# Moving the operands of the matmuls to other SBUF addresses modulo 256 bytes

## The chip, the cores and the metric

The kernel runs on one core of one Trainium2 chip. The metric is device time in microseconds (us) from one launch, lower is better. Three runs of the kernel before gave 332.88, 333.24 and 334.3 us, median 333.24. The profile shows one further execution, which took 333.72 us; from its first to its last instruction it spans 331.9 us.

A word on names: PE is the matmul engine (TensorE), PEld its weight loads, ACT is ScalarE, DVE is VectorE, POOL is GpSimd, SP is the engine that issues the DMAs. SBUF is the on-chip memory from which the matmuls read both operands; PSUM is where they write. An SBUF address here is a byte offset inside a partition, the same in all 128 partitions.

## The reference

Linear attention with a quadratic feature map, and behind it a gated network whose gate mixes positions. Batch 4, 4 heads, 1088 positions, head width 32, model width 128, 512 hidden channels in each half.

```python
q_p, k_p = (phi(q), phi(k))                       # 64 features of 32 channels
num = einsum(q_p, sum_s k_p v); den = q_p . sum_s k_p + 1e-06
x = num / den                                     # [4, 1088, 128]
h = maximum(x @ w_in, 0.0)                        # [4, 1088, 1024]
u, v = (h[..., :512], h[..., 512:])
v_n = (v - mean(v)) / sqrt(var(v) + 1e-06)
v_s = einsum('ts,bsd->btd', w_spatial, v_n) + b_spatial[None, :, None]
out = (u * v_s) @ w_out                           # [4, 1088, 128]
```

The largest part is `v_s`: for each batch a product of 512 channels by 1088 positions with a 1088 by 1088 matrix W (`w_spatial`).

## The kernel before

Products that need fp32 accuracy are built from three fp32r matmuls. Each operand is split into a high part (a cast to fp32r) and a low part (the rest), and high x high, high x low and low x high are added up in PSUM. `mm3` (lines 420 to 423) does so for the small products. For `v_s` the same three come from `high` (lines 939 and 941) and `low` (lines 948 and 950).

How `v_s` is tiled (`main`, `spatial`): the 1088 source positions are 9 tiles `kt` of 128, the last one with 64 real rows; the 512 channels are 4 groups `d` of 128; the 1088 target positions are 3 pieces `c` of 424, 332 and 332 columns (`CH`). For one (batch, d, c) there are 26 matmuls into one PSUM bank: for each of the first eight `kt` the pair (weights `vh`, moving `wTh`), (weights `vl`, moving `wTh`), (weights `vh`, moving `wTl`), and for the ninth (`vh`, `wTh`) and one with 66 rows (`vx`, `wTl`) that brings the bias too. "Weights" is the operand that is loaded into the array (128 x 128 fp32, 512 bytes in each partition); the "moving" operand is streamed past it. Every matmul has its own weight load. 26 matmuls x 4 batches x 4 groups give 416 for each piece, 1248 in all.

The other fp32r matmuls go through `mm3`: the hidden half `u` (`hidden`, weights `wih0` and `wil0`, moving the attention's output `xh`, `xl`, PSUM tile `pu`), the output product (`out_mm`, weights `woh` and `wol`, moving the gated tiles `g`, or `r` for the last group of the last batch; PSUM tile `po`), the half `v` (`hidden_v`, weights `xh` and `xl`, moving `wih1` and `wil1`, 512 columns), and the attention's own projections (moving `r`).

The order of all instructions is made when the program is built: `Order.schedule` simulates the engines with the planner's costs (`C_MM`, `c_act` and so on), with due times, and with a table of numbers `LEADS`. No address goes into it.

Where the operands lie is decided by the dictionary `homes` and the function `place` in `tile_kernel`. W's high and low part share one tile `wT`; a row of it (one `kt`) takes `PITCH` = 1152 elements, and the pieces begin in it at `AT[c] + AHEAD` elements. `PITCH` is 4608 bytes, a multiple of 256, so each piece begins at the same address modulo 256 in every row, high or low. The same holds for the weights: each 128 x 128 tile takes 512 bytes. `AHEAD` is 4 elements, 16 bytes.

Of the kernel before, what the change touches and what calls it, by code (L numbers as in the profile page):

```python
# [9 lines left out]
F32 = mybir.dt.float32  # L10
F32R = mybir.dt.float32r
# [6 lines left out]
B, H, S, D, R = 4, 4, 1088, 32, 8  # L18
DM, DFF, DH = 128, 1024, 512
P = 128  # L20
NS = 9
SPAD = NS * P
NK = 8
ND = DH // P
# [3 lines left out]


CH = [(0, 424), (424, 332), (756, 332)]  # L30
LINE, AHEAD = 32, 4
AT = [0, 448, 800]
PITCH = 1152
BIAS = [(0, 8, 53), (8, 4, 83), (12, 4, 83)]

TW = (384, 384, 320)
# [9 lines left out]
SB_BUFS = {  # L46
    "pl": 6, "c": 3, "r": 4, "abT": 2, "kt": 3, "v": 3, "ka": 2, "kp": 3, "kvh": 1, "kvl": 1,
    "xh": 2, "xl": 2, "vt": 3, "mv": 3, "st": 6, "sm": 12, "rec": 2, "vh": 4, "vl": 4, "u": 3, "g": 3,
}
# [284 lines left out]
def c_act(n, psum=False, ptr=False):  # L334
    return (157 if psum else 190) + 0.833 * n + (190 if ptr else 0) if n > 16 else 203


def c_dve(n):
    return 152 + 1.045 * n
# [6 lines left out]
def c_pool(n):  # L346
    return 90 + 2.4 * n
# [10 lines left out]
def tile_kernel(ctx: ExitStack, tc: tile.TileContext, kT, qT, vA, sks, idn, msk, wT, w_in, w_out, bsp, out):  # L358
# [7 lines left out]
    const = ctx.enter_context(tc.tile_pool(name="const", bufs=1))  # L366
    ps = ctx.enter_context(tc.tile_pool(name="ps", bufs=1, space=PSUM))

    homes = {
        "vh": const.tile([P, NS, ND, P], F32R, name="vh"),  # L370
        "vl": const.tile([P, NK, ND, P], F32R, name="vl"),
        "wiu": const.tile([P, 2, DH], F32R, name="wiu"),
        "wo": const.tile([P, 2, ND, DM], F32R, name="wo"),
        "wT": const.tile([P, 2 * NS * PITCH], F32R, name="wT"),
        "g": const.tile([P, SB_BUFS["g"], AT[1]], F32R, name="g"),
        "r": const.tile([P, SB_BUFS["r"] * 384 + 4 * AHEAD], F32R, name="r"),
        "x": const.tile([P, 2, SB_BUFS["xh"], SPAD], F32R, name="x"),
        "wiv": const.tile([P, 2 * DH + AHEAD], F32R, name="wiv"),
    }
    homes |= {("g", i): homes["g"][:, i, AHEAD:] for i in range(SB_BUFS["g"])}  # L380
    homes |= {("r", i): homes["r"][:, AHEAD + 384 * i:AHEAD + 384 * (i + 1)] for i in range(SB_BUFS["r"])}
    homes |= {(t, i): homes["x"][:, n, i] for n, t in enumerate(("xh", "xl")) for i in range(SB_BUFS[t])}
    fixed = {
        "wih0": homes["wiu"][:, 0], "wil0": homes["wiu"][:, 1], "woh": homes["wo"][:, 0], "wol": homes["wo"][:, 1],
        "wih1": homes["wiv"][:, AHEAD:AHEAD + DH], "wil1": homes["wiv"][:, AHEAD + DH:],
    }

    def place(t):
        if t.name in ("wTh", "wTl"):
            at = NS * PITCH * (t.name == "wTl")  # L390
            return homes["wT"][:, at:at + NS * PITCH].rearrange("p (k c) -> p k c", c=PITCH)
        if t.name in fixed:
            return fixed[t.name]
        if t.tag is None:
            return const.tile(t.shape, t.dt, name=t.name)
        if t.tag in ("vh", "vl"):
            return homes[t.tag][:, :, t.slot]
        if t.tag in ("kt", "v"):
            if t.tag not in homes:
                homes[t.tag] = const.tile([P, k.bufs(t.tag), k.size(t.tag)], t.dt, name=t.tag)  # L400
            homes[t.tag, t.slot] = homes[t.tag][:, t.slot]
        if (t.tag, t.slot) not in homes:
            pool = ps if t.tag in PS_BUFS else const
            homes[t.tag, t.slot] = pool.tile([P, k.size(t.tag)], t.dt, name=f"{t.tag}{t.slot}")
        home = homes[t.tag, t.slot]
        assert home.dtype == t.dt, t.tag
        home = home[:, :math.prod(t.shape[1:])]
        if len(t.shape) == 2:
            return home
        d = "abc"[:len(t.shape) - 1]  # L410
        return home.rearrange(f"p ({' '.join(d)}) -> p {' '.join(d)}", **dict(zip(d, t.shape[1:])))
# [3 lines left out]
    op, tl = k.op, k.tile  # L415
# [9 lines left out]
    def load(t, ap, src, kb, w=None, **kw):  # L425
        if t.name in FIRST:
            kw["due"] = FIRST.index(t.name) - 1e4
        op("SP", 470, lambda: nc.sync.dma_start(out=ap(), in_=src), w=[w or t], kb=kb, **kw)
# [27 lines left out]
    for par in range(ND):  # L456
        t = tl(None, f"v9{par}", [P, P], F32R)
# [40 lines left out]
    def split(hi, lo, x, n, r, wh, wl, pool=False, due=None, alt=False):  # L498

        op("ACT", c_act(n), lambda: nc.scalar.copy(out=hi(), in_=x()), r=r, w=wh)  # L500
        if pool:
            op("POOL", c_pool(n), sub_pool(lo, x, lambda: hi().bitcast(F32)), r=[*r, *wh], w=wl, due=due)
        else:
            alts = [("POOL", c_pool(n), sub_pool(lo, x, lambda: hi().bitcast(F32)))] if alt else []
            op("DVE", c_dve(n), sub(lo, x, lambda: hi().bitcast(F32)), r=[*r, *wh], w=wl, due=due, sh=True, alts=alts)
# [17 lines left out]
    woh = tl(None, "woh", [P, ND, DM], F32R)  # L523
    wol = tl(None, "wol", [P, ND, DM], F32R)
# [14 lines left out]

    def load_w(kt, c):  # L540
        c0, cw = CH[c]
        cs = slice(AT[c] + AHEAD, AT[c] + AHEAD + cw)
        raw = tl("pl", f"wt{kt}{c}", [P, cw])
        load(raw, lambda: raw[:, :cw], wT[kt * P:(kt + 1) * P, c0:c0 + cw], cw // 2)

        n = 64 if kt == NS - 1 else P
        op("ACT", c_act(cw), lambda: nc.scalar.copy(out=wTh[:, kt, cs], in_=raw[:, :cw]), r=[raw], w=[(wTh, (kt, c))])

        def low(eng):
            return lambda: eng.tensor_tensor(out=wTl[:n, kt, cs], in0=raw[:n, :cw], in1=wTh[:n, kt, cs].bitcast(F32), op=ALU.subtract)  # L550

        op("POOL", c_pool(cw), low(nc.gpsimd), r=[raw, (wTh, (kt, c))], w=[(wTl, (kt, c))], alts=[("DVE", c_dve(cw), low(nc.vector))], sh=True, kind=f"W{c}")

    def load_bias():
        b32 = tl(None, "b32", [83, 16])
        load(b32, lambda: b32.ap, bsp, 4)
        bh, bl = tl(None, "bh", [83, 16], F32R), tl(None, "bl", [83, 16], F32R)
        split(lambda: bh.ap, lambda: bl.ap, lambda: b32.ap, 16, [b32], [bh], [bl])
        for c, (at, w, rows) in enumerate(BIAS):
            for n, t in enumerate((bh, bl)):  # L560
                cs = slice(AT[c] + AHEAD, AT[c] + AHEAD + w * rows)
                op(
                    "SP", 470,
                    lambda n=n, t=t, cs=cs, at=at, w=w, rows=rows: nc.sync.dma_start(out=wTl[64 + n:65 + n, NS - 1, cs].bitcast(F32).rearrange("p (a c) -> p a c", c=w), in_=t[:rows, at:at + w].bitcast(F32)),
                    r=[t], w=[(wTl, ("bias", c, n))], kb=2,
                )
# [258 lines left out]
    def main(b, st):  # L825
# [4 lines left out]
        def big(c):  # L830

            return c == 0 and (wide or not b)
# [101 lines left out]
        def high(d, c, sp, kt):  # L934

            vh, vl, vx = hl[d]
            cw = cols[c][1]
            cs = slice(AT[c] + AHEAD, AT[c] + AHEAD + cw)
            nc.tensor.matmul(sp[:, :cw], vh[:, kt], wTh[:, kt, cs], start=(kt == 0), stop=False)  # L939
            if kt < NK:  # L940
                nc.tensor.matmul(sp[:, :cw], vl[:, kt], wTh[:, kt, cs], start=False, stop=False)  # L941

        def low(d, c, sp, kt):
            vh, vl, vx = hl[d]
            cw = cols[c][1]
            cs = slice(AT[c] + AHEAD, AT[c] + AHEAD + cw)
            if kt < NK:
                nc.tensor.matmul(sp[:, :cw], vh[:, kt], wTl[:, kt, cs], start=False, stop=False)  # L948
            else:
                nc.tensor.matmul(sp[:, :cw], vx[:66], wTl[:66, kt, cs], start=False, stop=True)  # L950
# [22 lines left out]
        def gate(d, c, sp, u):  # L973
            cw = cols[c][1]
            op("DVE", c_dve(cw), lambda: nc.vector.tensor_tensor(out=u.ap, in0=sp[:, :cw], in1=u.ap, op=ALU.mult), r=[sp], w=[u], lead=LEAD[1])  # L975
            if big(c):
                g = tl(("xh", "xl")[d % 2], f"g{b}{d}{c}", [P, 2, AT[1]], F32R)
                parts = [(lambda: g[:, 0, :cw], (g, 0)), (lambda: g[:, 1, :cw], (g, 1))]
            else:
                tag = "r" if last(d) else "g"  # L980
                gh, gl = tl(tag, f"gh{b}{d}{c}", [P, cw], F32R), tl(tag, f"gl{b}{d}{c}", [P, cw], F32R)
                parts = [(lambda: gh.ap, gh), (lambda: gl.ap, gl)]
            (hi, wh), (lo, wl) = parts
            split(hi, lo, lambda: u.ap, cw, [u], [wh], [wl])
            return hi, lo, [wh, wl]
# [122 lines left out]
```

## Time and profile before

| | |
|---|---|
| three runs, median | 333.24 us |
| the profiled execution | 333.72 us |
| its span, first to last instruction | 331.9 us |
| DVE busy in the span | 200.8 us (61%) |
| ACT busy | 158.1 us (48%) |
| POOL busy | 59.5 us (18%) |
| HBM read, written | 13.78 MB, 2.23 MB |

The span lies inside the execution; the 1.8 us between them are start and end. A row of the costliest groups reads: line, engine, operation, written tile <- read tiles, shape, count, then busy time in us and mean duration of one in ns, then the idle time of the engine just before such instructions. A row of the timeline reads: start in us from the beginning of the span, duration in us, engine, line, operation, tiles, shape, count. Matmuls are pipelined: the next starts long before the one before it has ended, so what a matmul costs the stream is the distance from its start to the next start, here called its **step**, and not its duration.

### The profile page before, as it was taken

Reading aid. Unit: us, or ns where it says so; the run is one execution under the profiler, and the core shown is the slowest. Engines: PE = TensorE matmul, PEld = TensorE weight load, DVE = VectorE, ACT = ScalarE, POOL = GpSimd, SP = SyncE. Lnnn points to the kernel's source line nnn. Section 1 sums busy time; section 2 is a strip of 40 time slices with the busy share of each in tenths; the row PEclk is TensorE's granted clock in tenths of the full one; section 3 lists DMA queues with packets and bytes.
Section 4 is the critical chain, followed back from the end, with each engine's and each line's share of the span. In section 5 each row is a group of like instructions: output and inputs, shape, how many; then the busy total and the mean of one; then the engine's idle time right before and its main releaser. Section 6 shows DMA issues by size and latency. Waiting matters only on the chain.

```text
span 331.9 us, 6032 instructions
## 1 busy us (share of the span) xinstructions
PE 325.9 (98%) x2308; PEld 313.6 (94%) x2308; DVE 200.8 (61%) x449; ACT 158.1 (48%) x365; POOL 59.5 (18%) x69
## 2 busy tenths in 40 slices
PE   8999999999999999999999999999999999999996
PEld 7987999999999899999999999999999999999995
DVE  4899995553799873769984267897722341221212
ACT  2589865444566661576553445564331252111122
POOL 1000216654114143411231215201000000000000
PEclk9999999999999999999999999999999999999999
DMA  7831458666111167500150353000000010000001
GB/s 227 288 86 39 127 150 273 153 128 169 52 46 43 20 126 146 147 2 24 46 96 0 76 110 60 2 0 0 3 0 2 0 47 22 0 2 1 0 2 67
DMA packets 18365, 23.10 MB, mean 70 GB/s; under 512 B 3104, under 2 KB 18080, under 8 KB 18336
## 3 DMA queue, kind: packets, MB, share of 16 engines
q1 hardware_dynamic: 18336, 22.71, 27.2%
q8 instruction: 18, 0.29, 0.4%
q14 instruction: 11, 0.09, 0.1%
HBM read 13.78 MB, written 2.23 MB: 48 GB/s over the span
## 4 chain that ended last, share of the span: by engine, by line
PE 86%; DVE 4%; DMA 4%; ACT 3%; issue 1%; SPq 1%; DVEq 0%; ACTq 0%
PE sp L939 19%; PE sp L941 17%; PE sp L948 17%; PE sd L421 3%; PE sd L422 3%; PE sd L423 3%; PE pu L421 2%; DMA pl<-in_wT 2%; PE pu L422 2%; PE pu L423 2%; PE po L422 2%; PE sp L950 2%; PE po L423 2%; PE po L421 2%; PE sd L634 2%; PE sd L587 2%
## 5 line engine op out<-in xcount | busy, mean ns | idle before, releaser
L939 PE MATMUL sp<-wT,vh 128*128 128x332 f32 (+1 forms) x414 | 135.3, 327 | 0.0
L941 PE MATMUL sp<-wT,vl 128*128 128x332 f32 (+1 forms) x368 | 119.6, 325 | 0.0
L948 PE MATMUL sp<-wT,vh 128*128 128x332 f32 (+1 forms) x368 | 117.6, 325 | 0.0
L939 PEld LDWEIGHTS sp<-wT,vh 128*128 128x128 f32 x414 | 77.9, 188 | 1.3
L941 PEld LDWEIGHTS sp<-wT,vl 128*128 128x128 f32 x368 | 69.3, 188 | 0.7
L948 PEld LDWEIGHTS sp<-wT,vh 128*128 128x128 f32 x368 | 69.2, 188 | 0.4
L975 DVE TENSOR_TENSOR u<-sp,u 128x332 f32<-128x332 f32 (+1 forms) x40 | 20.5, 515 | 39.1 <-PE sp L950 27.5
L431 DVE TENSOR_TENSOR g<-u,g 128x332 fp32r<-128x332 f32 (+1 forms) x38 | 22.0, 580 | 26.0 <-PE po L422 19.2
L500 ACT CAST g<-u 128x332 fp32r<-128x332 f32 (+1 forms) x38 | 17.9, 485 | 40.5 <-DVE u L975 25.9
L931 ACT ACTIVATE u<-pu 128x332 f32<-128x332 f32 (+1 forms) x40 | 18.5, 463 | 36.7 <-PE pu L423 35.7
L797 DVE BATCH_NORM_STATS2 st<-vt 128x6 f32<-128x512 f32 x36 | 24.3, 689 | 5.3 <-ACT vt L795 5.1
L775 DVE RECIPROCAL c<-c 128x384 f32<-128x384 f32 (+1 forms) x9 | 21.8, 2417 | 9.1 <-ACT c L773 9.1
L795 ACT ACTIVATE vt<-sd 128x512 f32<-128x512 f32 x36 | 21.4, 601 | 11.4 <-PE sd L423 10.7
L744 POOL TENSOR_TENSOR pl<-pl,pl 128x384 f32<-128x384 f32 (+1 forms) x18 | 19.0, 1062 | 33.8 <-DMA pl<-abT 33.6
L434 POOL TENSOR_TENSOR r<-pl,r 128x384 fp32r<-128x384 f32 (+1 forms) x18 | 17.6, 983 | 37.6 <-ACT r L500 37.5
L857 ACT CAST vh<-vt 128x384 fp32r<-128x384 f32 x36 | 17.4, 510 | 14.4 <-DVE vt L817 8.3
L859 DVE TENSOR_TENSOR vl<-vt,vh 128x384 fp32r<-128x384 f32 (+1 forms) x36 | 20.2, 579 | 2.8 <-ACT vh L857 2.7
L817 DVE TENSOR_SCALAR vt<-vt,mv,sm 128x512 f32<-128x512 f32 x32 | 17.4, 580 | 0.0
L434 POOL TENSOR_TENSOR r<-c,r 128x384 fp32r<-128x384 f32 (+1 forms) x9 | 9.7, 1081 | 40.3 <-ACT r L500 40.3
L421 PE MATMUL pu<-x,wiu 128*128 128x332 f32 (+1 forms) x48 | 16.0, 334 | 0.7 <-ACT kp L931 0.7
L422 PE MATMUL pu<-x,wiu 128*128 128x332 f32 (+1 forms) x48 | 15.7, 327 | 0.0
L423 PE MATMUL pu<-x,wiu 128*128 128x332 f32 (+1 forms) x48 | 15.7, 326 | 0.0
(161 smaller groups left out, 523.9 us busy)
## 6 DMA issues: line engine op xcount, KB each, us to landing
pl<-in_wT SPq DMA_DIRECT2D x18, 166.0 KB, 2.4
v<-in_vA SPq DMA_DIRECT2D x12, 198.0 KB, 4.1
kt<-in_kT SPq DMA_DIRECT2D x12, 192.0 KB, 3.1
pl<-abT SPq DMA_DIRECT2D x12, 192.0 KB, 4.4
pl<-in_wT SPq DMA_DIRECT2D x9, 212.0 KB, 6.1
c<-in_qT SPq DMA_DIRECT2D x9, 192.0 KB, 3.3
pl<-abT SPq DMA_DIRECT2D x24, 72.0 KB, 3.5
out<-u SPq DMA_DIRECT2D x6, 166.0 KB, 1.8
```

The lines of the kernel that those rows point to most:

```text
L421: nc.tensor.matmul(o, ah, bh, start=start, stop=False)
L422: nc.tensor.matmul(o, ah, bl, start=False, stop=False)
L423: nc.tensor.matmul(o, al, bh, start=False, stop=stop)
L431: return lambda: nc.vector.tensor_tensor(out=o(), in0=a(), in1=bb(), op=ALU.subtract)
L434: return lambda: nc.gpsimd.tensor_tensor(out=o(), in0=a(), in1=bb(), op=ALU.subtract)
L775: op("DVE", 135 + 6.3 * n, lambda x32=x32, n=n: nc.vector.reciprocal(out=x32[:, :n], in_=x32[:, :n]), w=[x32])
L795: op("ACT", c_act(512, True), lambda pv=pv, t=t: nc.scalar.activation(vt[:, t], pv.ap, AF.Relu), r=[pv], w=[(vt, t)])
L797: op("DVE", 690, lambda stats=stats, t=t: nc.vector.bn_stats(out=stats.ap, in_=vt[:, t]), r=[(vt, t)], w=[stats])
L939: nc.tensor.matmul(sp[:, :cw], vh[:, kt], wTh[:, kt, cs], start=(kt == 0), stop=False)
L941: nc.tensor.matmul(sp[:, :cw], vl[:, kt], wTh[:, kt, cs], start=False, stop=False)
L948: nc.tensor.matmul(sp[:, :cw], vh[:, kt], wTl[:, kt, cs], start=False, stop=False)
L975: op("DVE", c_dve(cw), lambda: nc.vector.tensor_tensor(out=u.ap, in0=sp[:, :cw], in1=u.ap, op=ALU.mult), r=[sp], w=[u], lead=LEAD[1])
```

## The change

Only addresses change. Every engine has the same instructions in the same order with the same waits as before: 2032 on PE, 451 on DVE, 367 on ACT, 74 on POOL and 162 on SP, each with the same operation and shape. The names of some tiles are new, since two joint tiles are taken apart (`wiu` and `wo`), one (`wiv`) becomes two plain ones, and the tiles `r` have no placed home any more. Small tiles (`ka`, `b32`, `mask_sb`, `rec`) are allocated early, between the large ones, and so shift these.

The addresses modulo 256 of the two programs, in bytes:

| operand | before | after |
|---|---|---|
| weights `vh`, `wih0`, `woh` (high) | 128 | 96 |
| weights `vl`, `wil0`, `wol` (low) | 128 | 224 |
| weights `vx` (66 rows) | 160 | 224 |
| moving W, piece 0 (424 columns) | 144 | 32 |
| moving W, piece 1 (332) | 144 | 240 |
| moving W, piece 2 (332) | 16 | 240 |
| moving `xh`, `xl` for `u`: pieces 0, 1, 2 | 192, 96, 144 | 32, 192, 240 |
| moving `g`: 424 wide, 332 wide | 144 or 192, 144 | 32, 240 |
| moving `r` | 144 | 0, and 160 in one of four |
| moving `wih1`, `wil1`; their weights `xh`, `xl` | 208; 192 | 160; 32 |

```diff
-LINE, AHEAD = 32, 4
-AT = [0, 448, 800]
-PITCH = 1152
+AT = [0, 436, 820]
+PITCH, G_PITCH, G_AT = 1152, 448, {424: 0, 332: 52}
...
-    homes = {
-        "vh": const.tile([P, NS, ND, P], F32R, name="vh"),
-        "vl": const.tile([P, NK, ND, P], F32R, name="vl"),
-        "wiu": const.tile([P, 2, DH], F32R, name="wiu"),
-        "wo": const.tile([P, 2, ND, DM], F32R, name="wo"),
-        "wT": const.tile([P, 2 * NS * PITCH], F32R, name="wT"),
-        "g": const.tile([P, SB_BUFS["g"], AT[1]], F32R, name="g"),
-        "r": const.tile([P, SB_BUFS["r"] * 384 + 4 * AHEAD], F32R, name="r"),
-        "x": const.tile([P, 2, SB_BUFS["xh"], SPAD], F32R, name="x"),
-        "wiv": const.tile([P, 2 * DH + AHEAD], F32R, name="wiv"),
-    }
-    homes |= {("g", i): homes["g"][:, i, AHEAD:] for i in range(SB_BUFS["g"])}
-    homes |= {("r", i): homes["r"][:, AHEAD + 384 * i:AHEAD + 384 * (i + 1)] for i in range(SB_BUFS["r"])}
+    homes, fixed = {}, {}
+
+    def weights(*names):
+        for x in names:
+            if x in ("vh", "vl"):
+                homes[x] = const.tile([P, NS if x == "vh" else NK, ND, P], F32R, name=x)
+            else:
+                fixed[x] = const.tile([P, DH], F32R, name=x)
+
+    homes["ka", 0] = const.tile([P, 96], F32, name="ka0")
+    fixed["b32"], fixed["mask_sb"] = const.tile([P, 16], F32, name="b32"), const.tile([P, 6], F32, name="mask_sb")
+    weights("vh", "wih0", "woh")
+    homes["ka", 1] = const.tile([P, 96], F32, name="ka1")
+    weights("vl", "wil0", "wol")
+    homes["rec", 0] = const.tile([P, 3 * H], F32, name="rec0")
+    homes["wT"] = const.tile([P, 2 * NS * PITCH], F32R, name="wT")
+    homes["g"] = const.tile([P, SB_BUFS["g"], G_PITCH], F32R, name="g")
+    homes["x"] = const.tile([P, 2, SB_BUFS["xh"], SPAD], F32R, name="x")
...
-    fixed = {
-        "wih0": homes["wiu"][:, 0], "wil0": homes["wiu"][:, 1], "woh": homes["wo"][:, 0], "wol": homes["wo"][:, 1],
-        "wih1": homes["wiv"][:, AHEAD:AHEAD + DH], "wil1": homes["wiv"][:, AHEAD + DH:],
-    }
...
+        if t.tag == "g":
+            at = G_AT[t.shape[1]]
+            return homes["g"][:, t.slot, at:at + t.shape[1]]
...
-        cs = slice(AT[c] + AHEAD, AT[c] + AHEAD + cw)
+        cs = slice(AT[c], AT[c] + cw)
```

The last pair stands for four places: the load of W, the bias rows, `high` and `low`.

More of the change, by code (lines that the diff above doesn't have):

```diff
@@ L392, in place @@
         if t.name in fixed:
-            return fixed[t.name]
+            home = fixed[t.name][:t.shape[0]]
+            return home.rearrange("p (d m) -> p d m", d=ND) if len(t.shape) == 3 else home
+        if t.tag == "g":
+            at = G_AT[t.shape[1]]
+            return homes["g"][:, t.slot, at:at + t.shape[1]]
         if t.tag is None:
@@ L560, in load_bias @@
             for n, t in enumerate((bh, bl)):
-                cs = slice(AT[c] + AHEAD, AT[c] + AHEAD + w * rows)
+                cs = slice(AT[c], AT[c] + w * rows)
                 op(
@@ L937, in high @@
             cw = cols[c][1]
-            cs = slice(AT[c] + AHEAD, AT[c] + AHEAD + cw)
+            cs = slice(AT[c], AT[c] + cw)
             nc.tensor.matmul(sp[:, :cw], vh[:, kt], wTh[:, kt, cs], start=(kt == 0), stop=False)
@@ L945, in low @@
             cw = cols[c][1]
-            cs = slice(AT[c] + AHEAD, AT[c] + AHEAD + cw)
+            cs = slice(AT[c], AT[c] + cw)
             if kt < NK:
@@ L976, in gate @@
             if big(c):
-                g = tl(("xh", "xl")[d % 2], f"g{b}{d}{c}", [P, 2, AT[1]], F32R)
+                g = tl(("xh", "xl")[d % 2], f"g{b}{d}{c}", [P, 2, G_PITCH], F32R)
                 parts = [(lambda: g[:, 0, :cw], (g, 0)), (lambda: g[:, 1, :cw], (g, 1))]
```

## The prediction

> **What bounds the kernel now.** I read the busy shares of the page first, then the waits of PE, then the groups by shape.
>
> ```profile
> span 331.9 us, 6032 instructions
> PE 325.9 (98%) x2308; PEld 313.6 (94%) x2308; DVE 200.8 (61%) x449; ACT 158.1 (48%) x365; POOL 59.5 (18%) x69
> PEclk9999999999999999999999999999999999999999
> PE 86%; DVE 4%; DMA 4%; ACT 3%; issue 1%; SPq 1%; DVEq 0%; ACTq 0%
> ```
>
> PE is busy for 98% of the span at its full granted clock, and 86% of the chain that ended last is PE. From the waits of PE and the stage table:
>
> ```profile
> PE sd L444 <- DVE z L440: 1.3, 1, 1.3
> PE po L422 <- DVE g L431: 0.8, 2, 0.5
> PE pu L421 <- ACT kp L931: 0.7, 2, 0.4
> ...
> 44.00:125.00 81.00, 80.25 (x565) 76.98 (x564) 58.12 (x123) 46.27 (x111) 30.96 (x32) 1.00 0.49 117
> 125.00:190.00 65.00, 65.00 (x500) 62.51 (x499) 42.49 (x94) 33.33 (x78) 16.36 (x18) 1.00 0.30 66
> 250.00:300.00 50.00, 50.00 (x306) 49.69 (x305) 13.60 (x28) 12.57 (x29) 0.00 (x0) 1.00 0.03 12
> ```
>
> The three waits together are 2.8 us (1.3 + 0.8 + 0.7). In the stages from 44 us on (PE, PEld, DVE, ACT, POOL in that order) PE is covered all the time or nearly so. The other engines have slack; a change that lets DVE or ACT read elsewhere can move little here. What the end depends on is the **step** of a matmul, the distance from its start to the next.
>
> ```profile
> L939 PE MATMUL sp<-wT,vh 128*128 128x332 f32 x288 | 90.6, 315 | 0.0
> L941 PE MATMUL sp<-wT,vl 128*128 128x332 f32 x256 | 80.0, 312 | 0.0
> L948 PE MATMUL sp<-wT,vh 128*128 128x332 f32 x256 | 80.0, 312 | 0.0
> ```
>
> These 800, with 32 of line 950, are the 832 matmuls of pieces 1 and 2; piece 0 has 416. Their rows give durations (some 313 ns) that overlap, so I took the steps from the starts in the timeline. The k-th matmul of the trace is the k-th of the program, which tells each row's piece and addresses.
>
> The steps are not all alike. Piece 1, a stretch of 15, from the first start to the first matmul behind it; then another stretch of 15 of piece 1; then 15 and 18 of piece 0:
>
> ```profile
> 255.01 0.31 PE L939 MATMUL sp<-wT,vh 128*128 128x332 f32 x1
> ...
> 257.21 0.35 PE L421 MATMUL po<-g,wo 128*128 128x424 f32 x1
> ...
> 289.03 0.32 PE L939 MATMUL sp<-wT,vh 128*128 128x332 f32 x1
> ...
> 291.33 0.36 PE L421 MATMUL pu<-x,wiu 128*128 128x424 f32 x1
> ...
> 262.83 0.35 PE L939 MATMUL sp<-wT,vh 128*128 128x424 f32 x1
> ...
> 265.64 0.35 PE L421 MATMUL po<-g,wo 128*128 128x424 f32 x1
> ...
> 296.63 0.36 PE L939 MATMUL sp<-wT,vh 128*128 128x424 f32 x1
> ...
> 300.17 0.32 PE L421 MATMUL po<-g,wo 128*128 128x332 f32 x1
> ```
>
> Piece 1: 2.20 us / 15 = 146.7 ns, and 2.30 / 15 = 153.3 ns, with the same shape, the same addresses, and hardly another engine at work. Piece 0: 2.81 / 15 = 187 ns, and 3.54 / 18 = 197 ns (inside it 193 and 200 alternate). So there is a **short** and a **long** step, and once PE is in one of them it stays there for the stretch. Both short ones are whole multiples of 6.67 ns (22 and 28), and 153.3 is 23 of them: a start seems to wait for the next tick of that length. Piece 2 has a third pattern:
>
> ```profile
> 322.75 0.31 PE L939 MATMUL sp<-wT,vh 128*128 128x332 f32 x1
> ...
> 326.24 0.32 PE L421 MATMUL po<-g,wo 128*128 128x332 f32 x1
> ```
>
> 23 steps in 3.49 us are 152 ns. Pieces 1 and 2 have one width and differ in the moving address alone, 144 against 16 modulo 256, beside weights at 128 for both. So the address has a part in it.
>
> **The change part by part.** No instruction is added, removed or moved; no queue, no DMA and no wait. What the change can touch is the steps.
>
> Over the whole trace (each group from its first row here to its last, undisturbed steps only), piece 0 has 413 with a mean of 192.3 ns, piece 1 413 with 149.9 ns, and piece 2 410 with 151.4 ns:
>
> ```profile
> 32.56 0.35 PE L939 MATMUL po<-wT,vh 128*128 128x424 f32 x1
> 47.43 0.32 PE L939 MATMUL sp<-wT,vh 128*128 128x332 f32 x1
> ...
> 317.97 0.32 PE L950 MATMUL sp<-wT,v 66*128 66x332 f32 x1
> 318.12 0.35 PE L421 MATMUL pu<-x,wiu 128*128 128x424 f32 x1
> ...
> 322.55 0.36 PE L950 MATMUL sp<-wT,v 66*128 66x424 f32 x1
> ...
> 326.09 0.32 PE L950 MATMUL sp<-wT,v 66*128 66x332 f32 x1
> ```
>
> Over the short step that is (192.3 - 186.7) x 416 = 2.3 us, (149.9 - 146.7) x 416 = 1.3 us, and (151.4 - 146.7) x 416 = 2.0 us: 5.7 us (of the sums before rounding) for W. For the gated tiles and the `u` half (48 groups of three each) the same count gives 0.4 and 0.9 us: their means are 150.6 ns (332 wide) and 190.4 (424) for `g`, and 149.3 (piece 2), 152.6 (piece 1) and 192.9 (424 wide at address 192) for `x`. Together 7.0 us, and **this is all that addresses can give if no step falls below the short one**, which no stretch of the trace does.
>
> The other end: every step long. Piece 0 at 196.7 costs (196.7 - 192.3) x 416 = 1.8 us, pieces 1 and 2 at 153.3 cost 1.4 and 0.8 us, the `g` and `x` ones some 0.8 us: 4.8 us more.
>
> Between these ends I have to place the new addresses. What counts for a step seems to be how the moving read and the next weight read stand to each other, modulo 256. Besides pieces 1 and 2 one place of the trace speaks for the weights' side: at the end of each stretch of piece 1 the last full matmul loads `vx`, at 160 and not at 128.
>
> ```profile
> 317.52 0.31 PE L941 MATMUL sp<-wT,vl 128*128 128x332 f32 x1
> 317.67 0.31 PE L948 MATMUL sp<-wT,vh 128*128 128x332 f32 x1
> 317.82 0.31 PE L939 MATMUL sp<-wT,vh 128*128 128x332 f32 x1
> ```
>
> The steps from 317.52 and 317.67 are 0.15 each by the rows (147 and 146 ns exactly), those from 317.82 and 317.97 are 153 and 154 ns. The moving address is unchanged; 32 bytes in the next weights, or their 66 rows, make the step long.
>
> Count the distance moving minus next weights, modulo 256. Before, it is 16 in pieces 0 and 1 and 144 in piece 2, the same at every step of a stretch. After, pieces 1 and 2 have 240 - 224 = 16 ahead of a low tile and 240 - 96 = 144 ahead of a high one (two of three steps): **the same two distances as before, but taken in turn**. Of steps at distance 16, 212 of 416 were short; at 144, 66 of 416; so both admit the short step. The long pattern of 153.3 was seen only where every step is at 16, the one of 152 only where every step is at 144. With the two in turn neither can repeat itself, while the short one can hold in both. My choice is that they regain half of their excess: mean 148.3 in piece 1 and 149.0 in piece 2.
>
> Piece 0 after has the distances 32 - 224 = 64 and 32 - 96 = 192. The nearest row is the 424-wide `x` at 192 beside weights at 128 (distance 64):
>
> ```profile
> 318.12 0.35 PE L421 MATMUL pu<-x,wiu 128*128 128x424 f32 x1
> 318.31 0.36 PE L422 MATMUL pu<-x,wiu 128*128 128x424 f32 x1
> 318.51 0.35 PE L423 MATMUL pu<-x,wiu 128*128 128x424 f32 x1
> 318.70 0.36 PE L939 MATMUL sp<-wT,vh 128*128 128x424 f32 x1
> ```
>
> 0.58 us for three, 193 ns, and 192.9 is the mean of all 70: no better than piece 0 now, but always three at a time, too few to settle. The alternation of 193 and 200 that costs piece 0 most needs equal distances too; so here also I take half, 189.5 ns, and keep 193 as the other end. `g` and `x` follow W.
>
> **Sum**: half of 7.0 us is 3.5 us. 333.72 - 3.5 = 330.2 us for an execution such as the profiled one, and as that lies 0.5 us over the median of the three runs, **329.7 us**. The 512-wide products (`wih1`), `r`, and the operands of DVE, ACT and POOL also move; I cost them at nothing. For the engines the cover is PE's full stream: DVE has 200.8 busy us of 331.9. The 512-wide steps are 232 ns now in 101 undisturbed ones; a tick of 6.67 ns on all 108 would be 0.7 us either way. Once steps are shorter, PE asks for its inputs sooner by 3 us in 330; waits of 2.8 us in the whole span say these would be in time, or give back some tenths.
>
> [...]
>
> **The rivals.**
>
> *All short.* Addresses chosen so that every read meets its tick at once: -7.0 us, 333.72 - 7.0 - 0.5 = 326.2 us. For it: stretches of 15 to 26 short steps exist at both distances. Against: piece 0's new distances show 193.
>
> *The distances decide one by one.* The mean of a step belongs to its own distance, taken in turn or not: pieces 1 and 2 become (149.9 + 2 x 151.4) / 3 = 150.9 against 150.7 now (+0.2 us over 832), piece 0 192.9 against 192.3 (+0.25 us): 333.24 + 0.45 = 333.7 us, no change that can be told. [...] For it: the 66 in 416 short steps of piece 2, hardly a stable pattern.
>
> *The short step needs one distance throughout.* As with `vx`, where a shift of the next weights ended it: with distances in turn no short stretch holds, and all steps of pieces 1 and 2 settle at 153.3 (+1.4 + 0.8 us), piece 0 at 193 to 197 (+0.3 to 1.8), the rest at +0.8 in the worst case: 335.7 to 338.0 us. It decides from the point where the mean W step grows by 1.3 ns (1.67 us, 0.5%, over 1248). Against it: only if `vx`'s address and not its 66 rows made that step long.
>
> **How the numbers follow.** Half regained, around 329.7 us: 0.42. All or nearly all short, 326.2: 0.10. No change, 333.7: 0.25. Longer, 335.7 to 338.0: 0.23. A measurement of this kernel can tell about 0.5%, 1.7 us: faster is under 331.6, slower over 334.9. Faster 0.52, same 0.25, slower 0.23. The range reaches from 326.0 to 336.2, which leaves out the worst half of the longer case. The forecast's own range is 328 to 331.5.
>
> **What would show it.** In the profile after, I look at the same starts: stretches of 332-wide matmuls near 146.7 ns per step with few at 153.3 (right), or a steady 152 to 153 (the slower rival); for 424 wide 187 against 193 to 197. PE's waits should stay near 3 us and DVE's and ACT's busy times within 1 us. I am wrong if piece 0 alone gets worse by more than pieces 1 and 2 gain, or if a step settles at a whole further tick (160 or 200 ns).

## The result and the profile after

The changed kernel takes 331.51 us (median of eight runs, 330.25 to 332.12) against 333.37 us for the kernel before beside it on the same chip (eight runs, 332.88 to 334.36). The ratio is 0.9937, with a 95% interval of 0.9916 to 0.9958: 2.1 us faster, between 1.4 and 2.8. The profiled execution took 331.01 us. Two executions of this study that took far longer, 458 us of the kernel before and 823 us of the first experiment's kernel, are left out of all medians and ratios.

The page of the kernel after, with the lines that answer to those shown of before:

```profile
span 329.2 us, 6032 instructions
PE 323.0 (98%) x2308; PEld 311.2 (95%) x2308; DVE 200.3 (61%) x449; ACT 158.0 (48%) x365; POOL 59.4 (18%) x69
PEclk9999999999999999999999999999999999999999
PE 76%; DVE 9%; ACT 5%; DMA 5%; SPq 2%; issue 1%; DVEq 0%; ACTq 0%
```

PE's busy time fell from 325.9 to 323.0 us and the span by 2.7 us. PE is still covered for 98% of the span, at a granted clock of 1.00 (before: 0.999). DVE, ACT and POOL are within half a microsecond of before. The chain shows PE with 76% where it had 86%: it runs through other instructions, but the idle time of PE hardly grew, as its waits show (engine, line, waited for, then us in total, times, longest):

```profile
PE sd L448 <- DVE z L444: 1.3, 1, 1.3
PE po L426 <- DVE g L435: 0.9, 2, 0.6
PE pu L425 <- ACT kp L935: 0.8, 2, 0.6
```

These are the same three as before, 3.0 us against 2.8. The lines of the kernel after are 4 further on: 943, 945, 952 and 954 are W's matmuls, 425 to 427 are `mm3`. Its groups by shape answer to the three of before, with one 424-wide group beside them:

```profile
L943 PE MATMUL sp<-wT,vh 128*128 128x332 f32 x288 | 90.1, 313 | 0.0
L952 PE MATMUL sp<-wT,vh 128*128 128x332 f32 x256 | 79.7, 311 | 0.0
L945 PE MATMUL sp<-wT,vl 128*128 128x332 f32 x256 | 79.6, 311 | 0.0
L943 PE MATMUL sp<-wT,vh 128*128 128x424 f32 x126 | 44.4, 352 | 0.0
```

The 332-wide ones are each 0.3 to 0.5 us shorter for the same count, and the 424-wide one, 44.7 us before, is 0.3 us shorter. Durations overlap, so the steps are again taken from the starts in the timeline. A whole stretch of 26 matmuls that is 332 wide and one that starts badly, then a stretch of 17 that is 424 wide; the last row of each is the first matmul behind it:

```profile
311.67 0.31 PE L943 MATMUL sp<-wT,vh 128*128 128x332 f32 x1
...
315.19 0.31 PE L943 MATMUL sp<-wT,vh 128*128 128x332 f32 x1
315.34 0.31 PE L954 MATMUL sp<-wT,v 66*128 66x332 f32 x1
315.49 0.36 PE L425 MATMUL pu<-x,wih 128*128 128x424 f32 x1
...
289.53 0.31 PE L943 MATMUL sp<-wT,vh 128*128 128x332 f32 x1
...
291.04 0.31 PE L945 MATMUL sp<-wT,vl 128*128 128x332 f32 x1
...
293.39 0.36 PE L425 MATMUL po<-x,woh 128*128 128x424 f32 x1
...
283.09 0.35 PE L943 MATMUL sp<-wT,vh 128*128 128x424 f32 x1
...
286.28 0.32 PE L425 MATMUL pu<-x,wih 128*128 128x332 f32 x1
```

The first takes 3.82 us / 26 = 147 ns a step, short from end to end. The second takes 1.51 us for its first 10 steps (151 ns) and 2.35 us for the other 16 (147 ns): it begins in the long pattern and leaves it. In after each of the 26 unbroken 332-wide stretches of 12 steps or more comes to a short step after 0 to 9 steps. In before 14 of 26 such stretches never have three short steps together, and none of its 32 unbroken rows of five or more 332-wide steps that are not short is followed by a short one (in after 17 of 31 are). The third is 3.19 / 17 = 188 ns.

Over the whole trace, counting undisturbed steps only (those up to 20 ns over the short one), and "short" as at most 148 ns (332 wide) or 188 ns (424 wide):

| W's steps | before | after |
|---|---|---|
| 332 wide (832): mean | 150.7 ns | 148.9 ns |
| short ones | 278 | 500 |
| steps in rows of 12 or more without a short one | 246 | 12 |
| 424 wide (416): mean | 192.3 ns | 190.2 ns |
| short ones | 147 | 214 |

W's steps give (150.66 - 148.93) x 832 = 1.4 us and (192.29 - 190.23) x 416 = 0.9 us, 2.3 us together. That carries the measured 2.1 us. The difference between the two profiled executions is larger, 2.7 us, because in after's the first fp32r matmul starts earlier, at 19.04 us (before: 19.88 us). That start lay anywhere from 19.0 to 20.7 us in the traces read for this study; the two of the kernel before alone have 19.88 and 19.41 us.

```profile
19.04 0.48 PE L425 MATMUL sd<-wih,x 128*128 128x512 f32 x1
```

### The profile page after: what moved, and what is told of

Its sections match the earlier page's. It is cut to its first block, busy times and chain, and to the rows that moved or that the text cites. A ratio compares the mean times of both kernels' runs of the same rounds, so it can differ in the third digit from the quotient of the medians.

```text
span 329.2 us, 6032 instructions
## 1 busy us (share of the span) xinstructions
PE 323.0 (98%) x2308; PEld 311.2 (95%) x2308; DVE 200.3 (61%) x449; ACT 158.0 (48%) x365; POOL 59.4 (18%) x69
## 4 chain that ended last, share of the span: by engine, by line
PE 76%; DVE 9%; ACT 5%; DMA 5%; SPq 2%; issue 1%; DVEq 0%; ACTq 0%
PE sp L943 18%; PE sp L945 16%; PE sp L952 16%; PE sd L425 3%; PE sd L426 3%; PE sd L427 3%; PE po L426 2%; DMA pl<-in_wT 2%; PE pu L425 2%; SPq L432 2%; DVE wT L554 2%; PE pu L427 2%; PE pu L426 2%; PE po L427 2%; PE po L425 2%; PE sd L638 2%
## 5 line engine op out<-in xcount | busy, mean ns | idle before, releaser
L425 PE MATMUL pu<-x,wih 128*128 128x332 f32 (+1 forms) x48 | 16.0, 334 | 0.8 <-ACT kp L935 0.8
L426 PE MATMUL pu<-x,wih 128*128 128x332 f32 (+1 forms) x48 | 15.7, 327 | 0.0
L427 PE MATMUL pu<-x,wil 128*128 128x332 f32 (+1 forms) x48 | 15.7, 327 | 0.0
```

The lines of the kernel that those rows point to most:

```text
L425: nc.tensor.matmul(o, ah, bh, start=start, stop=False)
L426: nc.tensor.matmul(o, ah, bl, start=False, stop=False)
L427: nc.tensor.matmul(o, al, bh, start=False, stop=stop)
```

## The experiments

The change moves the high weights, the low weights, the moving W, and the other moving operands. What counted for the forecast is the **distance**, the moving address minus the next weights' address modulo 256; the modulus is the author's choice, and no run tests it. The experiments give W other distances and leave the rest alone as far as the allocation allows. All compute the whole result. Times are medians; each kernel was compared with runs of the kernel before on the same chip.

**1. After, with all weights at 96.** The turn between two distances is gone: 332 wide nearly always at 240 - 96 = 144, 424 wide at 32 - 96 = 192 (the few steps into `vx` and into other products differ).

```diff
     weights("vh", "wih0", "woh")
-    homes["ka", 1] = const.tile([P, 96], F32, name="ka1")
     weights("vl", "wil0", "wol")
+    homes["ka", 1] = const.tile([P, 96], F32, name="ka1")
```

> The changed kernel with the low weights at 96 like the high ones; moving addresses stay, so the distance (moving minus next weights, modulo 256) is 144 at nearly every 332-wide step and 192 at every 424-wide one. Theory of turns (a step depends on the distance, and distances taken in turn break the lasting long patterns): W 332 goes back from 148.9 ns to about 151.4, as piece 2 of the kernel before; 424 at one distance can lock, 190 to 196 ns; time 332.5 to 334. Rival, only the moving address counts: 148.9 and 190.2 ns stay, 331.5 us.

332.50 us, median of eleven runs, ratio 0.9967 (0.9953 to 0.9982). The same kernel ran once more, on another chip, for a profile of it:

> The kernel with all weights at 96 once more, for an undisturbed profile of it. Theory of turns: W 332 at distance 144 throughout about 151.4 ns, like piece 2 of the kernel before (few short steps); its time of 332.56 us against 331.51 asks for some 1 us more of steps than in the changed kernel. Rival, each distance has its own mean: with 151.27 ns measured at distance 16 throughout, 148.93 would need 147.8 here.

331.36 us in that one execution, beside 333.39 us of the kernel before on that chip. A 332-wide stretch of 26 and a 424-wide one of 18 in its timeline:

```profile
311.92 0.32 PE L943 MATMUL sp<-wT,vh 128*128 128x332 f32 x1
...
315.88 0.36 PE L425 MATMUL pu<-x,wih 128*128 128x424 f32 x1
...
294.56 0.35 PE L943 MATMUL sp<-wT,vh 128*128 128x424 f32 x1
...
297.93 0.32 PE L425 MATMUL po<-g,woh 128*128 128x332 f32 x1
```

3.96 / 26 = 152 ns from the first step to the last, as in before's piece 2 at distance 144: the long pattern is back. Over the trace the 332-wide mean is 150.5 ns, with 241 steps in long rows, as before the change. But the 424-wide stretch is 3.37 / 18 = 187 ns, and their mean is 188.7 ns with no turn at all, better than after's 190.2. So here the turn serves the 332-wide pieces (148.9 against 150.5 ns); for piece 0 the distance 192 by itself does better than after's two (188.7 against 190.2).

**2. After, with all weights at 224.** The other distance alone: 332 wide always at 16, 424 wide always at 64.

```diff
-    weights("vh", "wih0", "woh")
     homes["ka", 1] = const.tile([P, 96], F32, name="ka1")
+    weights("vh", "wih0", "woh")
     weights("vl", "wil0", "wol")
```

> The changed kernel with the high weights at 224 like the low ones: distance 16 at every 332-wide step, 64 at every 424-wide one. Theory of turns: W 332 about 149.9 ns with stretches of 146.7 and of 153.3, as piece 1 of the kernel before; 424 around 193, the mean of the 424-wide hidden products at 64 before; time 332.5 to 333.5. Rival, only the moving address counts: 148.9 and 190.2 ns, 331.5 us. Rival, each distance has its own mean: (2 x the mean of the run with all weights at 96 + this one) / 3 gives the changed kernel's 148.9.

334.80 us, ratio 1.0039 (1.0022 to 1.0055): slower than before. A 332-wide stretch of 15, a 424-wide one of 17, and two of its groups:

```profile
290.40 0.32 PE L943 MATMUL sp<-wT,vh 128*128 128x332 f32 x1
...
292.70 0.36 PE L425 MATMUL pu<-x,wih 128*128 128x424 f32 x1
...
286.65 0.35 PE L943 MATMUL sp<-wT,vh 128*128 128x424 f32 x1
...
289.94 0.31 PE L425 MATMUL pu<-x,wih 128*128 128x332 f32 x1
```

```profile
L943 PE MATMUL sp<-wT,vh 128*128 128x332 f32 x288 | 90.9, 316 | 0.8 <-DVE kp L979 0.8
L943 PE MATMUL sp<-wT,vh 128*128 128x424 f32 x126 | 44.9, 357 | 0.0
```

2.30 / 15 = 153.3 ns, the long pattern of distance 16, and 3.29 / 17 = 193.5 ns at distance 64. Means 151.3 and 193.1 ns; the 424-wide group's mean duration went from after's 352 to 357 ns. The instructions, the moving addresses and their order are those of after, which takes 331.51 us: the place of the high weights (and of one small tile, `ka`, that was moved to shift them) is worth 3.3 us here.

**3. Before, with only the low weights moved 128 further.** `vl`, `wil0`, `wol` go from 128 to 0; W, `g`, `x`, `r` and the high weights stay where they were.

```diff
-        "vh": const.tile([P, NS, ND, P], F32R, name="vh"),
-        "vl": const.tile([P, NK, ND, P], F32R, name="vl"),
-        "wiu": const.tile([P, 2, DH], F32R, name="wiu"),
-        "wo": const.tile([P, 2, ND, DM], F32R, name="wo"),
...
+    homes["vh"] = const.tile([P, NS, ND, P], F32R, name="vh")
+    fixed = {x: const.tile([P, DH], F32R, name=x) for x in ("wih0", "woh")}
+    homes["ka", 0] = const.tile([P, 96], F32, name="ka0")
+    homes["vl"] = const.tile([P, NK, ND, P], F32R, name="vl")
+    fixed |= {x: const.tile([P, DH], F32R, name=x) for x in ("wil0", "wol")}
+    homes["ka", 1] = const.tile([P, 96], F32, name="ka1")
```

> The kernel before with nothing but the low weights (vl, wil0, wol) moved to 0 modulo 256, 128 past the high ones; all moving addresses as before. Piece 2 then has the distances 16, 144, 144 in turn as the changed kernel, pieces 0 and 1 have 144, 16, 16. Theory of turns: piece 2 falls from 151.4 to about 149, piece 1 has no lasting 153.3 any more and comes to 148 to 149.5, piece 0 loses its 193/200 and comes to 188 to 191; time 331 to 332. Rival, only the moving address counts: 149.9, 151.4 and 192.3 ns stay, 333.3 us.

331.71 us, ratio 0.9932 (0.9912 to 0.9952): **the whole gain of the change**. A 332-wide stretch of 26 (here lines 938 to 949 are W's):

```profile
313.17 0.32 PE L938 MATMUL sp<-wT,vh 128*128 128x332 f32 x1
...
317.02 0.35 PE L420 MATMUL pu<-x,wih 128*128 128x424 f32 x1
```

3.85 / 26 = 148 ns. Pieces 1 and 2 have 149.1 ns each, with no long row left (0 steps against 246); piece 0, here in turn between 16 and 144, has 191.0.

**4. After, with the pieces at 240, 240 and 48, and the weights as after.** Pieces 0 and 1 turn between 16 and 144, piece 2 between 80 and 208.

```diff
-AT = [0, 436, 820]
-PITCH, G_PITCH, G_AT = 1152, 448, {424: 0, 332: 52}
+AT = [4, 452, 788]
+PITCH, G_PITCH, G_AT = 1152, 448, {424: 4, 332: 4}
...
-    homes["rec", 0] = const.tile([P, 3 * H], F32, name="rec0")
     homes["wT"] = const.tile([P, 2 * NS * PITCH], F32R, name="wT")
     homes["g"] = const.tile([P, SB_BUFS["g"], G_PITCH], F32R, name="g")
+    homes["rec", 0] = const.tile([P, 3 * H], F32, name="rec0")
```

> The changed kernel with W at 224 modulo 256 and the pieces at 240, 240 and 48: piece 0 has the distances 16, 144, 144 in turn and not 64, 192, 192; piece 1 stays; piece 2 gets 80, 208, 208. Theory of turns: any two distances in turn break the locks, so piece 0 stays at 189 to 191 ns, piece 1 at 148.9, piece 2 at 148.5 to 151; time 331 to 332.5. Rival, the pair of distances itself counts: piece 0 or piece 2 moves by over 1.5 ns from 190.2 or 148.9, some 0.6 us for each.

333.12 us, ratio 0.9979 (0.9959 to 0.9999). Piece 1 keeps 148.6 ns and piece 0 has 190.0, but piece 2 has 152.3, with a single short step in 409. To be in turn was not enough here: 80 and 208 gave 152.3 ns where 16 and 144 gave 148.6.

**5. Everything of after 64 further.** W, `g`, `x`, the 512-wide operands and the weights that they meet all move by 64, `r` stays; no distance within a stretch of W changes.

```diff
+    homes["rec", 1] = const.tile([P, 3 * H], F32, name="rec1")
     homes["ka", 0] = const.tile([P, 96], F32, name="ka0")
```

> The changed kernel with vh, vl, wih0, wil0, woh, wol, W, g and x all 64 bytes further: all distances as in the changed kernel, all addresses different. Theory that only distances count: W 332 at 148.9 plus or minus 0.4 ns, 424 at 190.2 plus or minus 0.7, time 331.5. Rival, addresses themselves count: a mean moves by over 1 ns, time by about 1 us.

331.34 us, ratio 0.9933 (0.9911 to 0.9956), means 148.8 and 190.3 ns: after's within 0.2 ns. A shift of both sides by 64, which keeps their distance, left the means where they were.

**6. Before, in turn by the moving side.** W's low part moves 128 further, the weights stay. The distances are 16 and 144 again, but now a step's moving address differs from the one before it.

```diff
-        "wT": const.tile([P, 2 * NS * PITCH], F32R, name="wT"),
+        "wT": const.tile([P, 2 * NS * PITCH + 32], F32R, name="wT"),
+        ("ka", 0): const.tile([P, 96], F32, name="ka0"),
...
-            at = NS * PITCH * (t.name == "wTl")
+            at = (NS * PITCH + 32) * (t.name == "wTl")
```

> The kernel before with W's low part moved 128 bytes on and all weights left at 128: the turn comes from the moving side. Pieces 0 and 1 have the distances 16, 16, 144, piece 2 144, 144, 16. Theory of turns: it does not matter which operand moves: W 332 at 148.6 to 149.5 ns, 424 at 189.5 to 191.5, time 331.3 to 332 us. Rival, the high and low weight loads themselves must lie 128 apart (the loads disturb each other, not the moving read): no gain, 149.9, 151.4 and 192.3 ns, 333.4 us.

334.85 us, ratio 1.0042 (1.0027 to 1.0057): slower. A stretch of 26, 332 wide:

```profile
291.85 0.31 PE L940 MATMUL sp<-wT,vh 128*128 128x332 f32 x1
...
295.83 0.36 PE L422 MATMUL po<-x,wo 128*128 128x424 f32 x1
```

3.98 / 26 = 153 ns, and the means of pieces 1 and 2 are 152.7 and 151.7 ns with 107 short steps of 823 (before: 278). The same two distances, reached by moving the other operand, lose 0.42% here where moving the weights gained 0.68% (experiment 3).

**7. Three scans of distances.** `vh` and `vl` get room between the four channel groups, so that each group's weights lie 544 bytes on from the last and each (group, piece) has a distance of its own. Fewer buffers (`pl`, `u`) pay for the room, which costs time elsewhere: 348.23, 346.83 and 347.28 us in one execution each, at a granted clock of 0.985, 0.99 and 0.99 (0.999 to 1.0 in the other profiled executions). Only the steps are read from them, some 70 to 120 for each distance.

```diff
-        "vh": const.tile([P, NS, ND, P], F32R, name="vh"),
-        "vl": const.tile([P, NK, ND, P], F32R, name="vl"),
+        "vh": const.tile([P, NS, 576], F32R, name="vh"),
+        "vl": const.tile([P, NK, 576], F32R, name="vl"),
...
-            return homes[t.tag][:, :, t.slot]
+            return homes[t.tag][:, :, 136 * t.slot:136 * t.slot + P]
```

The first has the pieces of before and so distances of 16 plus multiples of 32; the second, with `AHEAD = 0` and `AT = [0, 464, 816]`, multiples of 32; the third is experiment 3 with this room and `AT = [8, 452, 804]`, so that each pair of distances is taken in turn.

The diff is the first scan's, against before.

> The kernel before with the four channel groups' weights 544 bytes apart and not 512 (at 128, 160, 192, 224), and two kinds of buffers fewer to make room, so that its order and its time are its own; the steps are what is read. Within a stretch the distance is constant: 16, 240, 208, 176 for pieces 0 and 1, 144, 112, 80, 48 for piece 2. Theory of turns with distances that admit the short step and others that do not: 16 and 144 show short steps, 80 and 208 hardly any (as piece 2 of the run with piece 0 at 240); 240, 176, 112 and 48 open. Rival, all constant distances are alike: means within 1 ns of each other.

> As the scan of distances, high and low weights alike, with W 16 bytes off: piece 0 at 64, piece 1 at 128, piece 2 at 0, so the constant distances are multiples of 32 (0, 224, 192, 160 for piece 1; 128, 96, 64, 32 for piece 2; 192, 160, 128, 96 for piece 0). Theory as it stands now (each constant distance has lasting patterns of its own, by the width): 424 wide at 192 is short nearly throughout, 187 to 189 ns, as in the kernel with all weights at 96; 332 wide open, 146.7 to 153.3. Rival, that run's 188.6 ns was a chance of its execution: 424 at 192 comes out at 191 to 195 here.

> As the scan of distances, but the low weights 128 past the high ones in every channel group: pieces 1 and 2 have the pairs 16/144, 240/112, 208/80 and 176/48 in turn, piece 0 (moved to 160) 32/160, 0/128, 224/96 and 192/64. Theory (weights in turn leave only a pattern that lasts at both distances): 16/144 at 148.5 to 149.5 ns with most steps short; 240/112, where both showed short steps when constant (49 of 99, 34 of 89), under 150 and shorter than either alone (149.9, 150.9); 208/80 without short steps, 152 to 153; 176/48 hardly any, 151.5 to 153; 192/64 for 424 wide near 190. Rival, low loads 128 past high ones help by themselves at any distance: all four pairs of the 332-wide pieces come to 148.5 to 150.

| 332 wide, the same distance throughout | mean, ns |
|---|---|
| 16, 192, 240 | 148.9, 149.2, 149.9 |
| 144, 112, 32, 0 | 150.8, 150.9, 151.1, 151.4 |
| 176, 80, 224, 48, 208 | 151.5, 151.5, 152.2, 152.5, 152.7 |
| 128, 64, 96, 160 | 153.2, 153.2, 153.3, 154.0 |

| 332 wide, two distances in turn | mean of piece 2 and of piece 1, ns |
|---|---|
| 16 and 144 | 148.0 and 149.5 |
| 80 and 208 | 151.6 and 152.0 |
| 48 and 176 | 152.4 and 152.4 |
| 112 and 240 | 153.6 and 151.9 |

For 424 wide, the same distance throughout: 192 gives 189.4, 16 gives 190.3, and the other six 191.1 (176) to 194.3 (96). The two pieces of a pair differ in which distance they take at two steps of three. In turn, 424 wide: 64 and 192 give 189.9; the pairs 32/160, 0/128 and 96/224 give 192.1 to 193.5. The last scan was expected to bring 112/240 under 150 ns, since both admit short steps alone; it did not. Of the four pairs only 16 and 144 came under 150 ns in both pieces.

**8. Before once more, and the good pair for all pieces.** A second profile of the kernel before, unchanged; and experiment 4 with piece 2 at 112, so that all three pieces turn between 16 and 144 (the diff is against experiment 4).

```diff
-AT = [4, 452, 788]
+AT = [4, 452, 804]
```

> The kernel before once more, unchanged, for a second profile of it: how far do the mean steps of W vary between executions where the patterns can last? With constant distances which pattern a stretch falls into hangs on how it is entered, so the means may differ by up to 1 ns: piece 1 149 to 151.3, piece 2 150.5 to 151.5, piece 0 191.5 to 193. If 332 wide came to 149 or less in both pieces, the gain of the change would be a chance of the one profile.

> The changed kernel with all three pieces of W and the gated tiles on the pair 16 and 144 (pieces at 240, 240 and 112). Theory: pieces 1 and 2 at 148.6 to 149.1 ns, piece 0 at 190 as in the run with piece 0 at 240, the 424-wide gated products near 190 where the changed kernel has 192.8: 0.2 to 0.3 us less than the changed kernel, 331.2 us, which cannot be told from it; clearly under the kernel before, ratio near 0.993. If piece 2 does not come down from 152.3 (its value at 80 and 208), the pair is not what counts.

Before again took 333.58 us, with 150.0, 151.6 and 191.9 ns for pieces 1, 2 and 0, 264 steps in long rows (246 in the first profile): within 0.4 ns of the first profile's 149.9, 151.4 and 192.3, so the patterns are not a chance of one execution. What decides which of them a single stretch falls into isn't shown. The other took 331.45 us, ratio 0.9943 (0.9926 to 0.9959): no better than after. Its piece 2 is at 149.3 ns where experiment 4 had 152.3, by 64 bytes in one piece's place.

All kernels side by side. "From W's steps" is the mean of pieces 1 and 2 times 832 plus that of piece 0 times 416, less the same of before (205.3 us); "measured" is the ratio less one, times 333.4 us. In line 1 the steps are those of the later execution, the measured time that of the eleven runs.

| kernel | 332 wide, ns | 424 wide, ns | from W's steps, us | measured, us |
|---|---|---|---|---|
| before again | 150.8 | 191.9 | -0.1 | - |
| after | 148.9 | 190.2 | -2.3 | -2.1 |
| 1, all weights at 96 | 150.5 | 188.7 | -1.6 | -1.1 |
| 2, all weights at 224 | 151.3 | 193.1 | +0.8 | +1.3 |
| 3, only low weights moved | 149.1 | 191.0 | -1.8 | -2.3 |
| 4, piece 2 at 80/208 | 150.5 | 190.0 | -1.1 | -0.7 |
| 5, all 64 on | 148.8 | 190.3 | -2.4 | -2.2 |
| 6, W's low part moved | 152.2 | 192.2 | +1.2 | +1.4 |
| 8, all pieces 16/144 | 149.0 | 190.5 | -2.2 | -1.9 |

In each line the two agree within 0.6 us, with nothing fitted. In these kernels the time moved with W's steps, and by no more than 0.6 us with anything else that the addresses touch.

## Why the prediction was right

331.51 us lies in the range (326.0 to 336.2), which also holds no change at all, and just past the edge of the forecast's own (328 to 331.5); faster was the likeliest case. The direction is confirmed, and for pieces 1 and 2 the end of the long rows in turn (246 steps to 12); the size was too large, and the reason given for piece 0 was wrong, so that the gain of piece 0 (0.9 of the 2.3 us from W's steps) came in part by luck.

**PE's stream bounds the kernel, and the steps set it.** Right: same instructions, same waits within 0.2 us, and the table above. The upper bound held too: no lasting step fell below 146.7 ns (332 wide) or 186.7 ns (424 wide) in any trace that was read.

**With 16 and 144 in turn the lasting long patterns end and the short one holds.** Right for the weights' side: steps in long rows fell from 246 to 12, and to 0, 0 and 14 in experiments 3, 5 and 8; with one distance they came back (241 and 291 in experiments 1 and 2). Five kernels with the pair in turn have 148.6 to 149.3 ns. The same distances without the turn gave 149.9 to 151.6 ns in the kernels of this table, where the counts are large; one scan has 148.9 at constant 16, on 77 steps. But the step was stated as one about distances, and that is too broad. Experiment 6 has the same distances in turn and loses; the pairs 80/208, 48/176 and 112/240 gain nothing. What the runs support is: this pair, with the moving address the same from step to step.

**Half of the excess comes back.** It was 44% for the 332-wide pieces (1.4 of 3.3 us) and 37% for piece 0 (0.9 of 2.3 us), 2.3 us where the forecast has 2.85.

**Piece 0 gains because its distances are no longer equal.** The gain came, but this reason failed. Distance 192 throughout gives 188.7 ns (experiment 1) and 189.4 (the scan), better than after's 190.2 with two distances. And the alternation of 193 and 200, which was to need equal distances, stands in after itself. In the first stretch of piece 0 the weights are `vh` and `vl` strictly by turns, and so are the distances 64 and 192. The two rows of after that bound it, and below them two of experiment 1's kernel at 192 throughout, 45 steps apart:

```profile
31.84 0.36 PE L943 MATMUL po<-wT,vh 128*128 128x424 f32 x1
...
43.24 0.35 PE L943 MATMUL po<-wT,vh 128*128 128x424 f32 x1
```

```profile
32.33 0.35 PE L945 MATMUL po<-wT,vl 128*128 128x424 f32 x1
...
40.73 0.35 PE L943 MATMUL po<-wT,vh 128*128 128x424 f32 x1
```

After takes 11.40 us for 58 steps, 197 ns each, with 193 and 200 alternating all the way, as in before; experiment 1's kernel takes 8.40 / 45 = 187 ns. Behind that stretch, where at most every third step of after is at 64, its piece 0 has 189.2 ns (before: 191.6). So two distances by themselves did not end the long pattern there. That the order in which they come makes the difference is the author's reading; no run changes the order alone.

The rival "the distances decide one by one" isn't the mechanism either. (2 x 188.7 + 193.1) / 3 = 190.2 is what piece 0 of after measures, but by coincidence: its steps at 64 have 190.2 ns and not the 193.1 of experiment 2, those at 192 have 190.3 and not 188.7. In pieces 1 and 2 after's steps at 16 and at 144 have 148.8 and 148.9 ns, where the same distances throughout gave 151.3 (experiment 2) and 150.6 (experiment 1). The 193 ns read off the 424-wide `x` for distance 64 holds for long stretches of W too (193.1); for 192 it doesn't: in experiment 1's stretch of 18 above the first four steps take 190 ns each (0.76 us) and the other 14 take 186 ns (2.61 us).

**`g` and `x` follow W.** Mis-sized: forecast 0.65 us of gain, measured about 0.1 us of loss (424-wide `g` 190.4 to 192.8 ns, 424-wide `x` with `u` 192.8 to 193.1, 332-wide `g` 150.6 to 150.4). They stand three at a time. W's long 332-wide stretches in after took up to 9 steps to come to a short one, so three may have no time for it. This reason is the author's, argued from those stretches; no run tests it. This term makes a little over half (0.75 us) of the distance between the forecast's 3.5 us and the measured 2.1 us.

**The 512-wide products at nothing.** Right within 0.1 us: 232.1 to 231.2 ns on 108.

**The rival that ends slower: the short step needs one distance throughout.** Its mechanism is refuted by after itself and by experiment 3, where short stretches hold with distances in turn (26 steps at 147 and at 148 ns each); only the strict alternation in piece 0's first stretch went the way it says. Its support, the step into `vx` that was 153 ns long, falls too: after has `vx` at 224, and a short stretch ends with 147, 147 and 151 ns there (the steps up to the one from 315.34 in the rows above). So the 66 rows alone don't make that step long; the addresses differ between the two kernels. Yet slower was within reach by a mechanism that the prediction didn't list: the turn made by the moving side (1.0042), or weights all at 224 (1.0039).

**All short.** No run reached it. Piece 0 does best at 192 throughout and pieces 1 and 2 with two distances in turn, but the three share their weights, so no kernel here has both; and no version that ran is measurably better than after.

Three things stay open. Experiment 1 gave 332.50 us as a median and 331.36 us in its later single execution on another chip, 1.1 us apart, and why isn't known. No run tells what in the memory or the array makes 16 and 144 a good pair and the others not. And why 64 and 192 kept the long pattern where they alternated strictly (197 ns a step), and not where 64 came at every third step at most (189.2 ns), isn't known; for the 332-wide pieces no run tried the strict alternation.

## What to carry to other kernels

Where PE is full, take the step from start to start for each shape, and compare equal matmuls at different addresses: if one of them has two lasting values, the operands' places modulo 256 are worth a scan, since here moving one set of weights by 128 bytes was worth 0.7% (experiment 3) and the wrong move cost 0.4% (experiments 2 and 6). Read the distance between the moving operand and the next weights, for each width by itself, and try moving the weights before the moving operand: 0.9932 against 1.0042 here, for the same two distances. Look at the order in which high and low weights come, too: in after, 64 and 192 by strict turns kept the long pattern (197 ns a step), and in the order of the later stretches piece 0 had 189.2 ns. Count only on long stretches; groups of three gained nothing here (424-wide `g` 190.4 to 192.8 ns).

## What the runs showed of the hardware that was not expected

In the traces of before, after and experiments 3, 5 and 8 the starts of the short 332-wide steps (those of 146 and 147 ns) lie together when they are taken from the span's start, modulo 6.67 ns, the distance between the lasting steps of 153.3 and 146.7 ns, here called a tick. The mean resultant length is 0.91 to 0.95, where 1 is all at one point and 0 an even spread; in before, experiments 3 and 8 it is taken for each moving address by itself. Where in the 6.67 ns the starts lie differed with the moving address: in before 3.2 ns for piece 1 (200 steps) and 6.4 ns for piece 2 (52 steps), whose addresses are 128 bytes apart; 5.2 and 1.8 ns in experiment 3; 2.9 and 6.2 ns in experiment 8. In these three kernels the two places are 3.2 to 3.4 ns apart, about half a tick. In after, where both pieces are at 240, both lie at 2.7 ns (243 and 235 steps).

In experiment 6 the moving address changes by 128 from one step to the next. There only 107 of 823 undisturbed steps were short, and those of one moving address are spread over the tick (resultant lengths 0.3 and 0.6). That the two have one cause is the author's guess; no run shows it. With a constant moving address and one distance the two lasting steps of piece 1 in before are 22 and 23 ticks (146.7 and 153.3 ns). The 152 ns pattern at constant 144 is not a whole number: 22.8 ticks a step, and its steps of 151, 152, 151, 153 and 153 ns make 114 ticks only in fives. The runs don't say why a stretch at 23 ticks in before does not come to 22, nor why with the weights in turn it does.
